# A new order of the same 1088 steps in a one-core RWKV-6 plus SwiGLU kernel

## The chip, the cores and the metric

The kernel runs on one core of a Trainium2 chip. The metric is the device time of one execution in microseconds; lower is better.

## The reference

Inputs are `r`, `k`, `v`, `w` of shape (4, 8, 768, 48) (batch, heads, positions, head size), `u` of shape (8, 48), and the FFN's weights. First a linear attention with a decaying state runs over the 768 positions, then an RMS norm and a SwiGLU FFN:

```python
for t in range(S):
    cur = einsum('bhd,bhe->bhde', u[None] * k_t, v_t)
    y[:, :, t] = einsum('bhd,bhde->bhe', r_t, state + cur)
    state = w_t[:, :, :, None] * state + einsum('bhd,bhe->bhde', k_t, v_t)
x = y.transpose(0, 2, 1, 3).reshape(3072, 384)
xn = x / sqrt(mean(x * x) + 1e-6) * rms_g          # per row
g = xn @ w_gate                                     # 384 x 1536
out = (silu(g) * (xn @ w_val)) @ w_out              # 1536 x 384
```

All data in DRAM is float32; the matmuls run in bfloat16.

## The kernel before

The positions are cut into 6 superblocks `m` of 128. In a superblock, `j` = 0 to 3 are the four batches; a tile (m, j) is 128 positions times 8 heads of 48. The whole program is one list of steps, `PLAN`, that is written out once. Each word of it is a step: `name.m.j` and more indices, `@n` is the buffer or PSUM bank that it takes, and `/A`, `/V`, `/G` says ScalarE, VectorE or GpSimd for steps that can run on any of them. Each engine executes its own steps in the order of the list, and waits by itself for what a step reads and for the buffer that it overwrites. So the list fixes five queues: PE's, VectorE's (DVE), ScalarE's (ACT), GpSimd's (POOL) and that of SyncE (SP), which issues nearly all DMAs.

```python
for step in PLAN.split():
    env.step(step)
```

The steps of a tile (line numbers are those of the profile):

| step | what it does | engine |
|---|---|---|
| `ld.m.j.w/k/r/v` | load of one 192 KB tile (L303) | SP |
| `ln`, `cs`, `exp` | log of the decay, sums of logs along positions by a matmul with a mask (L391), exponential (L400; L397 and L398 for m = 4, 5) | ACT, PE, ACT |
| `rk` | r and k times their decays, to bf16 (L412) | DVE |
| `tr` and `tre`, or `trp` | transposes of that: on PE with a copy out (m = 0, 1), or by DMA for two tiles at once (m from 2 on, L417) | PE and DVE/ACT, or SP |
| `q`, `qm` | r times k for all pairs of positions (L437), causal mask (L440) | PE, DVE |
| `y` | the masked product times v, plus r times the state (L450, L453) | PE |
| `ruk1`, `ruk2`, `bs`, `yd`, `xa` | the term with u and its addition (L478, L482, L485, L490, L494) | POOL, POOL, DVE, POOL, DVE |
| `sq`, `rs`, `xn` | RMS norm of the tile (L498, L503, L364 or L366) | ACT, POOL, any |
| `xt` and `xe`, or `xep` | transpose of the normed tile: on PE with a copy out (m = 0, 1), or by DMA for two tiles (L520) | PE and DVE/ACT, or SP |
| `st`, `sn`, `dk`, `dke`, `dm` | state: k times v (L461), its addition (L467), the decay of the block and its product | PE, DVE, PE, ACT, any |
| `gv.m.g.i.g/v` | gate and value matmuls of block i of the FFN (L538); in m = 0 and 1 for two token groups g of two tiles each, 6 blocks of two columns of 128, later one group, 12 blocks | PE |
| `si`, `hm` | SiLU of the gate (L542), product with the value (L546) | ACT, DVE |
| `o.m.j.q` | a third of the output matmul of a tile (L554) | PE |
| `oo`, `od` | copy out of PSUM, store | DVE/ACT, SP |
| `warm` | a 512-column matmul whose result is not used (L525), 24 of them | PE |
| `tab` | load of ScalarE's function table, for log and exp or for SiLU (L347) | ACT |

The FFN's weights come in float32 as twelve pieces of 384 KB for gate and value (`ldw.p.g`, `ldw.p.h`, p = 2 * third of the rows + half of the columns) and six for the output (`ldwo`). They land in 7 staging slots (`@0` to `@6`) and are cast to bf16 in halves by `wc` and `wco` (L356 to L366); a slot is free for the next piece when both of its halves have been cast. Four of the slots lie in the buffer that holds `hm`'s result of superblock 1.

The inputs have two buffers for each of `w`, `r`/`k` and `v`: superblock m uses one and m + 1 the other, so superblock 1's loads wait for nothing but their turn in SP's queue, and those of m + 2 wait for the last reader of m.

Of the kernel before, what the change touches and what calls it, by code (L numbers as in the profile page):

```python
# [100 lines left out]
tab.le.0 ld.0.1.w@0 ld.0.1.k@0 ld.0.0.r ld.0.3.v@0 ld.0.0.w ln.0.1.1@0 ld.0.2.w ldu cs.0.1@0 ld.0.1.r ld.0.1.v  # L101
ld.0.0.k ln.0.0.1 ld.0.3.r ldg cs.0.0@2 ln.0.2.1 ld.0.3.w ub@4 exp.0.1 ld.0.3.k exp.0.0 vc.0.1.1@0/V ldw.2.h@0
ube/A vc.0.3.1/V rk.0.0@0 ruk1.0.0@0 ldw.5.g@1 rk.0.1 ruk1.0.1@1 tr.0.0@5 ld.0.2.v st.0.1@6 ruk2.0.1 tre.0.0@0/V
ld.0.0.v sn.0.1/A ln.0.3.1 bs.0.1 ldw.0.g@2 cs.0.3@2 wc.2.h.1/V wc.2.h.0/G ld.0.2.r cs.0.2@0 exp.0.3 q.0.0@4
ruk2.0.0 ld.0.2.k vc.0.2.1/A ldw.1.h@3 warm.0@7 ruk1.0.3@1 bs.0.0 exp.0.2 tr.0.1@6 rk.0.3@1 ldw.3.g@4 wc.5.g.1/G
qm.0.0@0 tre.0.1/A tr.0.3@2 ldw.4.h@5 yd.0.0@0 vc.0.0.1/A tre.0.3@1/V q.0.1@4 ldw.0.h@6 wc.0.g.0/A yd.0.1@1
rk.0.2 tab.si.1 warm.1 ruk2.0.3 ldw.1.g@0 q.0.3@2 qm.0.1@1 st.0.3@6 y.0.0@0 wc.0.g.1/G wc.5.g.0/A tr.0.2@1
wc.1.h.1/A xa.0.0@0 ldw.3.h@1 y.0.1@4 st.0.2@5 warm.2 xa.0.1@1 sq.0.0 ruk1.0.2@0 st.0.0@0 warm.3 wc.3.g.1/V
warm.4 sq.0.1 warm.5 warm.6 ruk2.0.2 warm.7 tre.0.2/A warm.8 qm.0.3@2 warm.9 ldw.5.h@2 rs.0.0 wc.1.h.0/A
wc.4.h.0/V wc.4.h.1/G q.0.2@2 xn.0.0@0/A ldw.4.g@3 bs.0.3 warm.10 wc.3.g.0/V y.0.3@4 xt.0.0@1 warm.11 rs.0.1  # L110
ldwo.0@5 bs.0.2 xn.0.1/A wc.1.g.0/V ldw.2.g@4 yd.0.2@2 xe.0.0@0/V wc.0.h.0/A wc.3.h.0/V xt.0.1@1 warm.12
yd.0.3@3 wc.1.g.1/A warm.13 qm.0.2@0 warm.14 xe.0.1/A ldwo.2@0 gv.0.0.4.g@1 ld.1.0.v@1 xa.0.3@2 warm.15
# [12 lines left out]
cs.1.0@0 vc.1.1.1/V o.0.1.0@7 rk.1.1@2 exp.1.0 cs.1.3@2 dke.1@0 rk.1.0 cs.1.2@4 dm.1.0/G tr.1.1@6 ld.2.1.k
exp.1.2 o.0.1.1 bs.1.1 ruk1.1.2@1 tre.1.1@2/V exp.1.3 tr.1.0@0 ld.2.3.r o.0.1.2 vc.1.2.1/V yd.1.1@4 tre.1.0/A
ld.1.3.v o.0.3.0@1 rk.1.2@1 dm.1.3/G ld.2.3.v rk.1.3 q.1.1@4 yd.1.0@0 ld.2.0.k qm.1.1@1 q.1.0@2 tr.1.3@6
dm.1.1/G tr.1.2@0 ld.2.2.r ruk2.1.2 o.0.3.1 qm.1.0@2 tre.1.2@0/A ld.2.3.w@0 o.0.2.0@4 dm.1.2/G tre.1.3/V
oo.0.1@1/A y.1.1@5 ld.2.0.r o.0.3.2 vc.1.3.1/A ruk1.2.1@0 xa.1.1@0 y.1.0@0 ld.2.2.k bs.1.2 sq.1.1 q.1.2@2
xa.1.0@1 oo.0.3@2/A rs.1.1 q.1.3@6 od.0.1 st.1.0@5 qm.1.2@0 sq.1.0 o.0.2.1 xn.1.1@0/A rs.1.0 o.0.2.2 qm.1.3@1  # L130
ruk1.1.3@1 xn.1.0/A xt.1.1@0 y.1.2@1 xe.1.1@1/A xt.1.0@2 ld.2.1.w ruk2.1.3 y.1.3@3 tab.si.2 xe.1.0/V st.1.1@0
ld.2.0.w gv.1.0.2.g@2 yd.1.2@1 bs.1.3 gv.1.0.2.v@6 ld.2.2.v si.1.0.2@0 yd.1.3@3 xa.1.2@3 gv.1.0.1.v@7 ld.3.3.w@1
sq.1.2 gv.1.0.4.g@2 ruk1.2.0@1 xa.1.3@2 gv.1.0.0.g@1 hm.1.0.2@1 ld.2.2.w sq.1.3 ruk2.2.1 oo.0.2@1/V gv.1.0.1.g@3
si.1.0.4@2 ld.2.3.k gv.1.0.3.g@6 rs.1.3 si.1.0.1@1 od.0.0 gv.1.0.0.v@4 ruk2.2.0 si.1.0.0@0 hm.1.0.1 gv.1.0.5.g@2
ld.3.1.w hm.1.0.0 rs.1.2 si.1.0.3@1 st.1.3@3 ld.3.0.w gv.1.0.3.v@1 xn.1.3@1/G sn.1.1 si.1.0.5@0 bs.2.1 st.1.2@4
tab.le.2 o.1.1.0@7 ld.3.2.w sn.1.0 ruk1.2.2@0 gv.1.0.4.v@6 hm.1.0.3 ld.3.2.k@1 ln.2.0.4@0 xt.1.3@0 gv.1.0.5.v@2
xn.1.2/G hm.1.0.4 bs.2.0 hm.1.0.5 xe.1.3/A ruk1.2.3@1 cs.2.0@5 sn.1.3 cs.2.1@0 exp.2.0 ld.3.1.k dk.2@2 sn.1.2
exp.2.1 rk.2.0@0 cs.2.3@3 ld.3.2.r o.1.1.1 dke.2@1 rk.2.1 exp.2.3 ld.2.1.v cs.2.2@5 dm.2.3/G o.1.0.0@2 exp.2.2
rk.2.3@2 trp.2.0@1 dm.2.2/G xt.1.2@0 o.1.1.2 xe.1.2/A ruk2.2.2 rk.2.2 tab.si.3 gv.1.1.1.g@1 ruk2.2.3 trp.2.1@2
gv.1.1.0.g@3 si.1.1.1@1 gv.1.1.2.g@0 dm.2.0/G bs.2.3 gv.1.1.1.v@6 oo.1.1@0/V si.1.1.2@2 dm.2.1/G gv.1.1.2.v@4  # L140
bs.2.2 od.1.1 si.1.1.0@0 hm.1.1.1 ruk1.3.2@1 gv.1.1.0.v@5 vc.2.0.4@0/A ld.3.1.v@1 hm.1.1.2 gv.1.1.3.g@7 yd.2.0@2
ld.3.1.r hm.1.1.0 q.2.0@0 si.1.1.3@1 yd.2.2@4 q.2.1@3 od.0.3 gv.1.1.4.g@6 qm.2.0@2 yd.2.1@0 gv.1.1.5.g@5
ld.3.3.v si.1.1.4@2 qm.2.1@0 y.2.0@7 ld.3.0.k yd.2.3@1 si.1.1.5@0 q.2.3@0 tab.le.3 q.2.2@5 xa.2.0@0 gv.1.1.3.v@3
qm.2.3@1 y.2.1@4 ruk1.3.1@0 sq.2.0 o.1.0.1 ld.3.0.v xa.2.1@1 ln.3.0.4@1 y.2.3@7 rs.2.0 qm.2.2@2 o.1.0.2 ld.3.2.v
st.2.1@4 sq.2.1 xa.2.3@2 ld.3.3.k y.2.2@0 xn.2.0@0/V gv.1.1.5.v@1 rs.2.1 sq.2.3 xa.2.2@3 ld.3.3.r gv.1.1.4.v@5
xn.2.1/V rs.2.3 sq.2.2 hm.1.1.5 cs.3.3@6 ld.3.0.r oo.1.0@0/A rs.2.2 o.1.3.0@0 hm.1.1.3 exp.3.3 xn.2.2@1/G sn.2.1
cs.3.1@1 xep.2.0@0 dk.3@3 hm.1.1.4 exp.3.1 st.2.0@4 o.1.3.1 xn.2.3/V dke.3@0 sn.2.0 xep.2.1 o.1.2.0@5
vc.3.0.4@1/A dm.3.1/G rk.3.1@1 cs.3.0@3 o.1.2.1 ruk2.3.1 rk.3.3@0 od.0.2 exp.3.0 o.1.3.2 dm.3.0/G bs.3.1
# [473 lines left out]
```

## Time and profile before

| | |
|---|---|
| four runs | 209.62, 208.83, 209.03, 211.1 us |
| median | 209.32 us |
| the profiled execution | 209.62 us |
| its span in the profile | 207.8 us, so 1.8 us lie around it |
| busy in the span | PE 189.2, DVE 151.5, ACT 132.8, POOL 115.7 us |
| DMA | 36.75 MB, 129497 packets, of these 123969 under 512 bytes |
| granted TensorE clock | 0.997 |

The profile is of one execution. A line of its timeline has start and duration in us, engine, source line, operation, what is written and read, the count, and in brackets how long the engine idled before and what it waited for. "SPq" are SyncE's DMA issues; a row for them lasts as long as the issue, not as the transfer. A row of the table by stretches has the length, then for PE, PE's weight loads, DVE, ACT and POOL the busy time and count, then the granted clock, the DMA engines' busy share and GB/s. The chain of waits has start, duration and what the end waited for in that time.

### The profile page before, as it was taken

To read this page: it belongs to the slowest core of one execution; us is meant where nothing else is said; L and a number is where in the kernel's file an instruction comes from. 1 tells how busy PE (TensorE), PEld (TensorE's weight loads), DVE (VectorE), ACT (ScalarE), POOL (GpSimd) and SP (SyncE) were. 2 spreads that over 40 slices of the span, in tenths; PEclk is the share of its full clock that TensorE was granted. 3 is DMA by queue.
4 is the path that set the end of the run, shared out by engine and by line. 5 is a ranking of instruction groups with operands and counts; after the bars stand their busy time and mean duration, and the time that the engine had idled before them with its cause. 6 is when DMAs were issued, how large, how long until landed. Compare 5 with 4: busy or idle time off the path is not lost.

```text
span 207.8 us, 4431 instructions
## 1 busy us (share of the span) xinstructions
PE 189.2 (91%) x1642; PEld 117.5 (57%) x1642; DVE 151.5 (73%) x252; ACT 132.8 (64%) x240; POOL 115.7 (56%) x144
## 2 busy tenths in 40 slices
PE   1437979899999989999999999999999999999993
PEld 0124738787677857876445565455664555544461
DVE  2065898477997798998999967799988986023731
ACT  3427778379748899899536988649994753333500
POOL 3059983053598969779866979739965141000000
PEclk9999999999999999999999999999999999999998
DMA  6999989999999997989999999999666307121113
GB/s 126 211 256 271 372 294 246 286 230 211 219 186 236 203 195 136 219 159 210 187 216 206 207 239 204 188 188 246 140 129 134 95 2 69 35 84 44 38 41 115
DMA packets 129497, 36.75 MB, mean 177 GB/s; under 512 B 123969, under 2 KB 127170, under 8 KB 129474
## 3 DMA queue, kind: packets, MB, share of 16 engines
q1 hardware_dynamic: 128928, 36.35, 79.1%
q8 instruction: 13, 0.21, 0.4%
q10 hardware_dynamic: 546, 0.10, 0.3%
q14 instruction: 10, 0.08, 0.1%
HBM read 25.96 MB, written 4.72 MB: 148 GB/s over the span
## 4 chain that ended last, share of the span: by engine, by line
PE 67%; DMA 9%; DVE 9%; SPq 8%; issue 3%; ACT 3%; POOL 1%; DVEq 0%; ACTq 0%; POOLq 0%
PE ps L538 38%; PE ps L554 18%; SPq L303 7%; DMA ht<-in_moe_w_out_dram 3%; PE ps L437 3%; DVE rkA L412 3%; DMA rkT<-rkA 2%; DMA ht<-in_moe_w_val_dram 2%; DMA in_rk<-in_r_dram 2%; PE ps L453 2%; DVE qts L440 2%; PE ps L391 1%; PE ps L450 1%; PE ps L461 1%; PE ps L425 1%
## 5 line engine op out<-in xcount | busy, mean ns | idle before, releaser
L542 ACT ACTIVATE sg<-ps 128x512 bf16<-128x512 f32 x72 | 41.9, 595 | 38.5 <-PE ps L538 27.8
L546 DVE TENSOR_TENSOR ht<-ps,sg 128x512 bf16<-128x512 f32 x72 | 47.8, 685 | 23.3 <-PE ps L538 16.9
L538 PE MATMUL ps<-xnt,wg 128*128 128x256 bf16 (+1 forms) x288 | 54.5, 326 | 0.5 <-ACT xnt L360 0.4
L538 PE MATMUL ps<-xnt,wv 128*128 128x256 bf16 (+1 forms) x288 | 54.7, 326 | 0.0
L554 PE MATMUL ps<-wo,ht 128*128 128x384 bf16 x288 | 53.3, 326 | 0.0
L478 POOL TENSOR_TENSOR ruk<-in_rk 128x384 f32<-128x384 f32 x24 | 24.2, 1011 | 28.4 <-DMA in_rk<-in_k_dram 19.4
L538 PEld LDWEIGHTS <-wg 128*128 128x128 bf16 x288 | 27.6, 98 | 18.0 <-issue 1.0
L538 PEld LDWEIGHTS <-wv 128*128 128x128 bf16 x288 | 27.2, 98 | 16.9
L554 PEld LDWEIGHTS <-ht 128*128 128x128 bf16 x288 | 26.9, 98 | 17.2 <-issue 0.2
L440 DVE TENSOR_TENSOR qts<-ps,mask_lt 128x1024 bf16<-128x1024 f32 x24 | 28.5, 1216 | 0.2 <-PE ps L437 0.2
L482 POOL TENSOR_TENSOR ruk<-ruk,u_bc 128x384 f32<-128x384 f32 x24 | 24.2, 1013 | 0.5
L412 DVE TENSOR_TENSOR rkA<-in_rk,ps 128x768 bf16<-128x768 f32 x24 | 22.2, 948 | 3.1 <-POOL in_rk L408 1.3
L503 POOL TENSOR_TENSOR rstd<-rstd,mhalf 128x1 f32<-128x1 f32 x24 | 13.8, 579 | 16.1 <-ACT junk L498 15.9
L490 POOL TENSOR_TENSOR ydr<-in_v,diag 128x384 f32<-128x384 f32 x24 | 19.7, 839 | 1.7 <-DVE diag L485 1.7
L472 POOL TENSOR_TENSOR st<-sf,wcr 128x384 bf16<-128x384 f32 x19 | 16.0, 845 | 6.4 <-ACT wcr L384 3.4
L498 ACT ACTIVATE junk<-xb 128x388 bf16<-128x388 bf16 x24 | 12.6, 524 | 6.8 <-DVE xb L494 6.4
L485 DVE TENSOR_REDUCE diag<-ruk 128x8 f32<-128x384 f32 x24 | 13.0, 545 | 4.2 <-POOL ruk L482 4.2
L347 ACT ACT_TABLE_LOAD x12 | 15.4, 1283 | 0.9 <-PEq L606 0.7
L494 DVE TENSOR_TENSOR xb<-ps,ydr 128x384 bf16<-128x384 f32 x24 | 13.1, 552 | 2.7 <-PE ps L453 2.2
L391 PE MATMUL ps<-lw,mask_nge 128*128 128x384 bf16 x16 | 5.8, 365 | 9.1 <-ACT lw L350 8.8
L400 ACT ACTIVATE ps<-ps 128x768 f32<-128x768 f32 x16 | 12.4, 793 | 2.4 <-PE ps L391 2.3
L350 ACT ACTIVATE lw<-in_w 128x384 bf16<-128x384 f32 (+1 forms) x12 | 9.8, 838 | 5.6 <-DMA in_w<-in_w_dram 5.5
(79 smaller groups left out, 211.4 us busy)
## 6 DMA issues: line engine op xcount, KB each, us to landing
in_w<-in_w_dram SPq DMA_DIRECT2D x24, 192.0 KB, 3.8
in_rk<-in_k_dram SPq DMA_DIRECT2D x24, 192.0 KB, 3.8
in_rk<-in_r_dram SPq DMA_DIRECT2D x24, 192.0 KB, 3.9
in_v<-in_v_dram SPq DMA_DIRECT2D x24, 192.0 KB, 3.9
out_dram<-obr SPq DMA_DIRECT2D x23, 192.0 KB, 2.7
ht<-in_moe_w_val_dram SPq DMA_DIRECT2D x4, 384.0 KB, 4.7
ht<-in_moe_w_gate_dram SPq DMA_DIRECT2D x4, 384.0 KB, 5.0
ht<-in_moe_w_out_dram SPq DMA_DIRECT2D x4, 384.0 KB, 4.8
```

The source lines that it names most:

```text
L303: self.nc.sync.dma_start(out=t, in_=getattr(self, w)[j, :, m * L:(m + 1) * L, :].rearrange("h t d -> t h d"))
L347: self.nc.scalar.preload_act_table_set(LN_EXP if kind == "le" else SILU)
L412: self.nc.vector.tensor_tensor(out=self.half("rkA", m, j)[:, :, :, 0:D], in0=self.in_rk[:, self.slot["in_rk", m], j], in1=self.b2(("cs", m ...
L440: self.nc.vector.tensor_tensor(out=self.qts[:, self.slot["qts", m, j]].rearrange("p a q t -> p (a q) t"), in0=self.b2(("qb", m, j)).rearra ...
L472: (self.nc.vector if eng == "DVE" else self.nc.gpsimd).tensor_tensor(out=self.st[:, m % 2, j].rearrange("p q (a d) -> p q a d", a=2), in0= ...
L478: self.nc.gpsimd.tensor_tensor(out=self.ruk[:, self.slot["ruk", m, j]], in0=rk[:, 0], in1=rk[:, 1], op=ALU.mult)
L482: self.nc.gpsimd.tensor_tensor(out=t, in0=t, in1=self.u_bc, op=ALU.mult)
L490: self.nc.gpsimd.tensor_tensor(out=self.ydr[:, self.slot["ydr", m, j]], in0=self.in_v[:, self.slot["in_v", m], j], in1=self.diag[:, m * SB ...
L538: self.nc.tensor.matmul(ps[:, a * n:(a + 1) * n].rearrange("p (u t) -> p u t", t=L), lhsT=w[:, c, f * 128:(f + 1) * 128], rhs=x[:, :, c], ...
L542: self.nc.scalar.activation(out=self.sg[:, self.slot["sg", m, g, i]], in_=self.b1(("gvb", m, g, i, "g")), func=AF.Silu)
L546: self.nc.vector.tensor_tensor(out=self.ht[:, self.slot["ht", m], fs[0]:fs[-1] + 1, t0:t0 + n], in0=self.b1(("gvb", m, g, i, "v")).rearran ...
L554: self.nc.tensor.matmul(ps, lhsT=self.ht[:, self.slot["ht", m], f, j * L:(j + 1) * L], rhs=self.wo[:, f, :], start=(f == 0), stop=(f == FC ...
```

## The change

The list of steps is replaced by another order of exactly the same 1088 steps: the former order was taken as the start of a search that went on for 900 seconds more, without building a first order anew from a list of priorities. Nothing else in the program differs. What changes with it: the order on each of the five queues, the bank or buffer of many steps, and the engine of 69 steps (for example `xn.0.0`, `xn.0.1` from ACT to DVE, `tre.0.0`, `tre.0.3` from DVE to ACT, `vc.0.0.1` from ACT to DVE, and 16 of the 24 `wc`). By engine, DVE has 9 `wc` instead of 11, 2 `tre` instead of 4, 14 `xn` instead of 10; ACT has 12 `wc` instead of 9; POOL has 3 `wc` instead of 4 and 5 `xn` instead of 7.

The diff of the head, up to the first `gv`:

```diff
-tab.le.0 ld.0.1.w@0 ld.0.1.k@0 ld.0.0.r ld.0.3.v@0 ld.0.0.w ln.0.1.1@0 ld.0.2.w ldu cs.0.1@0 ld.0.1.r ld.0.1.v
-ld.0.0.k ln.0.0.1 ld.0.3.r ldg cs.0.0@2 ln.0.2.1 ld.0.3.w ub@4 exp.0.1 ld.0.3.k exp.0.0 vc.0.1.1@0/V ldw.2.h@0
-ube/A vc.0.3.1/V rk.0.0@0 ruk1.0.0@0 ldw.5.g@1 rk.0.1 ruk1.0.1@1 tr.0.0@5 ld.0.2.v st.0.1@6 ruk2.0.1 tre.0.0@0/V
-ld.0.0.v sn.0.1/A ln.0.3.1 bs.0.1 ldw.0.g@2 cs.0.3@2 wc.2.h.1/V wc.2.h.0/G ld.0.2.r cs.0.2@0 exp.0.3 q.0.0@4
-ruk2.0.0 ld.0.2.k vc.0.2.1/A ldw.1.h@3 warm.0@7 ruk1.0.3@1 bs.0.0 exp.0.2 tr.0.1@6 rk.0.3@1 ldw.3.g@4 wc.5.g.1/G
-qm.0.0@0 tre.0.1/A tr.0.3@2 ldw.4.h@5 yd.0.0@0 vc.0.0.1/A tre.0.3@1/V q.0.1@4 ldw.0.h@6 wc.0.g.0/A yd.0.1@1
-rk.0.2 tab.si.1 warm.1 ruk2.0.3 ldw.1.g@0 q.0.3@2 qm.0.1@1 st.0.3@6 y.0.0@0 wc.0.g.1/G wc.5.g.0/A tr.0.2@1
-wc.1.h.1/A xa.0.0@0 ldw.3.h@1 y.0.1@4 st.0.2@5 warm.2 xa.0.1@1 sq.0.0 ruk1.0.2@0 st.0.0@0 warm.3 wc.3.g.1/V
-warm.4 sq.0.1 warm.5 warm.6 ruk2.0.2 warm.7 tre.0.2/A warm.8 qm.0.3@2 warm.9 ldw.5.h@2 rs.0.0 wc.1.h.0/A
-wc.4.h.0/V wc.4.h.1/G q.0.2@2 xn.0.0@0/A ldw.4.g@3 bs.0.3 warm.10 wc.3.g.0/V y.0.3@4 xt.0.0@1 warm.11 rs.0.1
-ldwo.0@5 bs.0.2 xn.0.1/A wc.1.g.0/V ldw.2.g@4 yd.0.2@2 xe.0.0@0/V wc.0.h.0/A wc.3.h.0/V xt.0.1@1 warm.12
-yd.0.3@3 wc.1.g.1/A warm.13 qm.0.2@0 warm.14 xe.0.1/A ldwo.2@0 gv.0.0.4.g@1 ld.1.0.v@1 xa.0.3@2 warm.15
...
+tab.le.0 ld.0.2.w@0 ld.0.1.w ld.0.0.w ld.0.1.k@0 ld.0.0.r ln.0.2.1@0 ld.0.3.w ldu ln.0.1.1 ld.0.3.v@0 cs.0.1@0
+ln.0.0.1 ld.0.2.k cs.0.2@2 ld.0.0.k exp.0.2 ld.0.1.v ub@4 ln.0.3.1 ld.0.3.r cs.0.0@6 ld.0.1.r exp.0.0 ld.0.3.k
+ldg exp.0.1 rk.0.0@0 ruk1.0.0@0 ld.0.2.v ube/V vc.0.1.1@0/A cs.0.3@6 ld.0.2.r ruk2.0.0 tr.0.0@5 exp.0.3
+ldw.0.h@0 rk.0.1 ruk1.0.1@1 tre.0.0@0/A ldw.5.g@1 rk.0.3@1 tr.0.1@4 ruk2.0.1 ldw.2.h@2 q.0.0@0 bs.0.1 tre.0.1/A
+ld.0.0.v vc.0.2.1/V ruk1.0.3@1 warm.0@5 vc.0.3.1/A ldw.0.g@3 qm.0.0@0 tr.0.3@6 tab.si.1 yd.0.1@0 ldw.1.g@4
+rk.0.2 ruk2.0.3 q.0.1@0 tre.0.3@1/A ldw.4.g@5 wc.0.h.0/V wc.5.g.0/G warm.1 bs.0.0 wc.0.h.1/A tr.0.2@7 ldw.3.g@6
+qm.0.1@1 wc.5.g.1/A ruk1.0.2@0 wc.2.h.0/A ldw.4.h@0 vc.0.0.1/V y.0.1@4 wc.2.h.1/A yd.0.0@1 xa.0.1@0 y.0.0@6
+ldw.2.g@1 st.0.3@2 ruk2.0.2 bs.0.3 warm.2 sq.0.1 warm.3 st.0.1@3 tre.0.2/V q.0.3@0 rs.0.1 xa.0.0@1 yd.0.3@2
+qm.0.3@2 q.0.2@6 sq.0.0 warm.4 warm.5 wc.0.g.0/A warm.6 ldwo.3@2 rs.0.0 warm.7 warm.8 wc.0.g.1/A xn.0.0@0/V
+xn.0.1/V xt.0.0@4 wc.1.g.0/A wc.4.g.1/V ldw.1.h@3 xt.0.1@0 warm.9 xe.0.0@0/V y.0.3@1 wc.3.g.0/A bs.0.2 warm.10
+st.0.2@4 warm.11 xe.0.1/A wc.4.h.0/V warm.12 wc.4.g.0/V warm.13 wc.3.g.1/A gv.0.0.3.g@0 wc.1.g.1/V ldw.3.h@5
...
```

SP's queue from the transposes of superblock 2 to those of superblock 3, read out of the two lists:

```
before: trp.2.0 trp.2.1 od.1.1 ld.3.1.v ld.3.1.r od.0.3 ld.3.3.v ld.3.0.k ld.3.0.v ld.3.2.v ld.3.3.k ld.3.3.r
        ld.3.0.r xep.2.0 xep.2.1 od.0.2 ld.4.1.k ld.4.0.k trp.3.0 trp.3.1
new:    trp.2.0 ld.3.1.k trp.2.1 ld.3.3.w ld.3.1.r ld.3.0.v ld.3.0.k od.1.1 ld.3.3.v ld.3.1.v ld.3.2.v od.0.2
        ld.3.3.r xep.2.0 ld.3.0.r xep.2.1 od.0.3 ld.4.0.k trp.3.0 trp.3.1
```

PE's order around `cs` of superblock 2:

```
before: xt.1.3 gv.1.0.5.v cs.2.0 cs.2.1 dk.2 cs.2.3 o.1.1.1 cs.2.2 o.1.0.0 xt.1.2 o.1.1.2 gv.1.1.1.g
new:    gv.1.0.4.v xt.1.3 cs.2.0 o.1.1.1 cs.2.1 cs.2.3 cs.2.2 dk.2 o.1.1.2 gv.1.1.2.g
```

On SP's queue, the last tile of superblock 3's `w` moves from place 70 of the 154 issues to place 77, and that of superblock 5 from 127 to 129 (counted from 0).

## The prediction

> **What bounds the kernel now.** I read the page first, then the busy time by stretch, then the instructions in order of time around the first FFN matmul, SyncE's DMA issues, and the chain of waits between 86 and 108 us. The page's second part:
>
> ```profile
> span 207.8 us, 4431 instructions
> ...
> PE   1437979899999989999999999999999999999993
> ...
> DMA  6999989999999997989999999999666307121113
> ```
>
> A slice is 5.2 us: PE is nearly full from the ninth on, and the DMA engines are full up to the 29th. The stretches say how much PE idles (first pair of numbers: length, PE busy):
>
> ```profile
> 0.00:31.00 31.00, 17.95 (x139) 10.22 (x140) 17.83 (x36) 17.15 (x29) 19.45 (x30) 1.00 0.97 256
> 31.00:100.00 69.00, 66.98 (x731) 51.82 (x729) 57.90 (x100) 54.84 (x96) 46.20 (x56) 1.00 0.97 210
> 100.00:204.30 104.30, 104.25 (x777) 55.48 (x774) 75.43 (x117) 60.51 (x114) 50.06 (x59) 1.00 0.65 134
> ```
>
> Idle PE is 13.05 us before 31 us, 2.02 us from there to 100 us, 0.05 us to the last matmul, and 3.5 us of output tail. The PE work is the same multiset of matmuls in both orders, so a reordering moves the end only by (a) the moment at which gv starts, (b) what PE work is left then, (c) the idle of the middle, at most 2 us to win, and (d) new stalls. The first gv:
>
> ```profile
> 30.16 0.46 ACT L360 COPY xnt<-ps 128x384 bf16<-128x384 bf16 x1
> ...
> 30.67 0.70 PE L538 MATMUL ps<-xnt,wg 128*128 128x256 bf16 x5 [0.44 <-ACT xnt L360]
> ```
>
> It waits for xe.0.1, not for a weight. The second bound is SyncE's queue, which issues every load in order: between 31 and 146 us it waits for data for only 0.4 us and then once more, before trp.2.0:
>
> ```profile
> 74.61 0.70 SPq L303 DMA_DIRECT2D in_v<-in_v_dram  x1
> 78.46 2.01 SPq L417 DMA_TRANSPOSE rkT<-rkA  x1
> ```
>
> That gap is 3.15 us. Elsewhere a load is late because the queue is full. The chain shows where this touches PE:
>
> ```profile
> 92.24 3.91 DMA in_rk<-in_r_dram
> ...
> 96.18 0.96 DVE rkA L412
> ...
> 102.52 4.33 DMA rkT<-rkA
> ...
> 106.90 0.40 PE ps L437 x8
> ```
>
> The last r tile of superblock 3 lands, rk and the DMA transpose follow, and q.3.2 starts as that transpose lands. A new order has to win at the head and must not lose it in this queue.
>
> **1. The head, up to the first gv.** Landings come one per 1.05 us (27 transfers from 3.48 to 30.67 us; 0.99 for the first twelve small ones, about 1.1 for a 384 KB weight). The new queue puts 15 of the 16 tiles of superblock 0 ahead of the weights, so I place: k00 11.4 us (as now), r01 14.4 (now 9.4), r02 17.3, then 0.h, 5.g, 2.h at 18.4 to 20.5, v00 21.2 (now 18.1), 3.g 25.7.
>
> VectorE, with start-to-start times of the rows (rk 0.87, qm 1.14, bs, xa and sn 0.47, tre 0.61, wc 0.33): rk.0.1 waits for r01 to 15.4, qm.0.0 17.3 to 18.5, qm.0.1 20.1 to 21.3, xa.0.1 22.5, xa.0.0 24.05; sq.0.0 (0.62) and rs.0.0 (0.6) bring xn.0.0 and xn.0.1, now both on VectorE, to 26.0. In the trace xn.0.1 is a ScalarE step that ends at 29.18, after rs.0.1 waited behind the 1.28 us cast wc.4.h.1 on GpSimd. Before xe.0.0, VectorE loses three weight casts (1.0 us), one tre (0.6) and bs.0.2 (0.5), and gains the two xn and ube (0.9). ScalarE casts 0.g, 1.g.0 and 3.g.0 (0.54 each) after sq.0.0 and ends xe.0.1 at 27.3. The first gv (0.0.3.g) needs 1.g.0, 3.g.0 and 5.g.0: all cast by 26.9.
>
> On PE, seven warm matmuls, y.0.3, st.0.2, xt.0.0 and xt.0.1 lie between q.0.2 (24.7) and gv, so their speed counts. [...] Row:
>
> ```profile
> 24.48 0.63 PE L525 MATMUL ps<-mask_lt 128*128 128x512 bf16 x1
> ...
> 25.23 1.97 PE L525 MATMUL ps<-mask_lt 128*128 128x512 bf16 x7
> ```
>
> The first of these spends 0.63 us, those after about 25.6 us come every 0.22. If this change of speed comes at 25.6 again, gv starts at **28.3**. [...] I take the row: 28.3, **-2.4 us**. [...]
>
> **2. Work left over.** st.0.0 and one more warm now come after the first gv: 0.17 + 0.22 = **+0.4**.
>
> **3. Middle, 31 to 75 us.** Stalls that go: 0.68 at 38.69 (VectorE stood before wco.5.0, waiting for its DMA, with xn.0.3 queued behind it; that cast is now ScalarE's), 0.34 at 57.88, and 0.73 + 0.2 + 0.2 around cs.2.0 to cs.2.2. What is late next, by the same walk: q.1.0 waits 0.2 for rk.1.3 and tre.1.0; cs.2.0 0.15 for ln.2.0 behind its table load; cs.2.2 now takes the bank of cs.2.0 and waits 0.6 for rk.2.0. Together 2.15 go and 0.95 come: **-1.2**. Bounds: 0 and -1.8. All of superblock 1's loads come without one of superblock 2 among them, the last (v12) at about 53.5 against 58.9 now, so ln.1.2 and rk.1.3 still find their data, by 1 us.
>
> [...] The trace shows both: the cast wc.3.h.0 took 0.95 beside GpSimd's yd.0.2, but wc.3.g.0 took 0.41 wholly inside GpSimd's wc.4.h.1. The new order has wc.1.g.1 on VectorE begin inside wc.2.g.1 on GpSimd (27.9 to 29.15), with qm.0.2 behind it and y.0.2 waiting. [...] The other swaps between engines (obr copies, vc, rw, dm) lie where PE has work queued, and cost nothing while that cover holds; without it each costs at most its own length, 0.3 to 1.5 us, once.
>
> **4. Superblock 2 to 3, on SyncE's queue.** Here the order loses. A load (31k) now stands between trp.2.0 and trp.2.1, and the last r tile (30r) comes behind xep.2.0 instead of ahead of it. With L for the lead gained so far: rk.2.3 ends at 81.1 - L, trp.2.1 has been issued at 83.9 - L (2.6 us each in this stretch), ten items follow as one per 1.0 us, xep.2.0 is reached at 93.9 - L, 30r is issued at 95.3 - L, and xep.2.1 at 96.3 - L lands (3.1 to 3.3) at 99.5 - L. gv.2.0.5.g follows st.3.0, which waits for rk.3.0 on 30r: about 100.2 - L, against 99.01 for the first gv.2.0 now. **+1.2**; ends 0 and +2. From there to the end both orders have 0.05 us or less to lose: y.5.0 to gv.5 has 9.3 us of other matmuls between, where the trace's chain took 7.6. **0**.
>
> Sum: -2.4 + 0.4 - 1.2 + 1.2 = -2.0. Against the profiled execution's own 209.62 (span 207.8 and 1.8 around it) that is 207.6; this execution lay 0.3 above the median of the four (209.32), so **207.3** as a median, 1.0% less. About 1% is also what a measurement of this kernel can tell from no change.
>
> **Rivals.**
> - *The queue gives nothing back* (step 4 is free, because 30r and the transposes find shorter queues as the DMA engines catch up): 207.3 - 1.2 = **206.1**. For it: in the trace SyncE waited 3.15 us at trp.2.0, so there is slack ahead of the place. Against: from trp.2.1 to xep.2.0 there was none.
> [...]
> - *v00 stops VectorE, slower.* vc.0.0.1 moves from ScalarE to VectorE and v00 from 16th to 19th transfer, behind three weights. VectorE has no spare time from there to the first gv; sq.0.0 follows, ScalarE's casts of 0.g are behind it, and ldw.1.h, which needs their stage slot, then blocks SyncE with all later loads behind it. Each us that v00 lands after 21.3 costs one us. At 1.05 us a transfer it lands in time; the gain is gone at 23.3 (1.10 us each), and at 1.2 to 1.25 us each, 25.6 us, the kernel is at 207.3 + 4.3 = **211.6**. For it: the last weights of the trace (4.g, 2.g) came 1.2 to 1.5 apart with stalls. Against: small tiles took 0.75 to 1.0.
> - That the change does not do what it says is no case here: only the list of steps changes.
>
> **How the numbers follow.** Forecast case 0.43, free queue 0.17, late speed-up 0.17, v00 0.23. The forecast lies at the edge of 1%: about half of its cases and all of the free queue are faster by over 1% (0.40), the other half, most of the late speed-up and a little of v00 are within 1% (0.37), and v00 is slower (0.23). The range takes in the free queue with the earliest gv (205.6) and the nearer half of the v00 case: 205.6 to 211.2.
>
> **What would show it.** Right: first gv at 27.9 to 29.6 us with xt.0.1 done before 28; v00 landing near 21.3; 31 to 75 us with about 1 us of idle PE; the first gv.2.0 at 96 to 97.5 us, waiting for rk.3.0 or for xnt by DMA, and SyncE waiting about 2 us before trp.2.0. Wrong: first gv after 30.7, idle PE of more than 1 us after 100 us, a wait at cs.3 or cs.5 for ln (their last w tiles now come late in the queue), or ScalarE as the releaser of long waits in the head.

## The result, and the profile after

| | old order | new order |
|---|---|---|
| median | 210.01 us (64 runs, 208.28 to 211.55) | 210.85 us (43 runs, 208.74 to 212.78) |
| profiled execution | 209.62 us | 210.78 us |
| its span | 207.8 us | 209.0 us |
| its last matmul ends at | 204.30 us | 204.41 us |
| from there to the end of the span | 3.54 us | 4.58 us |

The ratio of new to old is **1.0033** (95% interval 1.0017 to 1.0049): slower by a third of a per cent, where 1% less was forecast. Ratios are formed from the fast executions of each kernel alone, so they are not the quotients of the medians. The last two rows are the first finding: in this pair of executions the last matmul ends 0.11 us later, and 1.04 of the 1.16 us that were lost lie behind it, in a part that the prediction took as given.

The page of the new order (5.2 us to a digit, as before):

```profile
span 209.0 us, 4424 instructions
...
PE   0638789999999989999999999999999999999991
...
DMA  6999969999899969989999999899584303212022
```

The stretches that were shown of the old order, now of the new one (length, then busy time and count of PE, PE's weight loads, DVE, ACT, POOL, then granted clock, DMA share, GB/s):

```profile
0.00:31.00 31.00, 18.69 (x142) 11.14 (x143) 18.39 (x36) 19.10 (x31) 18.22 (x29) 1.00 0.93 247
31.00:100.00 69.00, 66.88 (x727) 51.18 (x727) 58.95 (x100) 57.13 (x100) 42.86 (x54) 1.00 0.99 216
100.00:204.30 104.30, 103.91 (x774) 55.23 (x772) 75.75 (x119) 56.37 (x110) 52.65 (x60) 1.00 0.62 132
```

PE does 0.74 us more before 31 us, idles 2.12 us instead of 2.02 in the middle, and 0.39 us instead of 0.05 after 100 us. The first gv starts at 28.78 us against 30.67; the idle PE after it sums to 3.26 us against 2.07. The timeline of the new order around it (start, length, engine, line, operation, what is written and read, count, and the idle time before with what ended it):

```profile
27.53 0.48 ACT L360 COPY xnt<-ps 128x384 bf16<-128x384 bf16 x1 [0.26 <-PE ps L513]
...
28.42 1.55 DVE L366 TENSOR_SCALAR wg<-stage_x,g_col 128x384 bf16<-128x384 f32 x2
...
28.78 0.82 PE L538 MATMUL ps<-xnt,wg 128*128 128x256 bf16 x6
...
28.83 0.92 POOL L490 TENSOR_TENSOR ydr<-in_v,diag 128x384 f32<-128x384 f32 x1
...
29.89 1.21 DVE L440 TENSOR_TENSOR qts<-ps,mask_lt 128x1024 bf16<-128x1024 f32 x1
...
31.15 0.81 PE L538 MATMUL ps<-xnt,wg 128*128 128x256 bf16 x6 [0.90 <-DVE qts L440]
```

xe.0.1 ends at 28.0 us and gv follows at 28.78 without idle PE: st.0.2 and three warm matmuls stand between. Then comes a new stall. The two casts on VectorE are wc.4.g.0 and wc.1.g.1; the second takes 0.98 us beside GpSimd's yd.0.2, so qm.0.2 ends at 31.10, and gv.0.0.0.g, which takes the bank that qm.0.2 reads, waits 0.90 us.

After 100 us there is one stall, and it comes from SyncE's queue:

```profile
127.01 3.01 SPq L417 DMA_TRANSPOSE rkT<-rkA  x1
...
130.06 0.58 SPq L562 DMA_DIRECT2D out_dram<-obr  x1
...
134.23 0.48 ACT L360 COPY obr<-ps 128x384 f32<-128x384 f32 x1 [2.77 <-DMA out_dram<-obr]
...
134.76 0.81 PE L538 MATMUL ps<-xnt,wv 128*128 128x512 bf16 x3 [0.39 <-ACT obr L360]
```

The issue of trp.4.0 lasts 3.01 us; the store od.1.3 stands behind it, lands at 134.20, and oo.2.0, which needs its buffer, holds ScalarE for 2.77 us and PE for 0.39.

### The profile page after: what moved, and what is told of

The parts are those of the page before. It is cut to its first block, busy times and chain, and to the rows that moved or that the text cites. A ratio compares the mean times of both kernels' runs of the same rounds, so it can differ in the third digit from the quotient of the medians.

```text
span 209.0 us, 4424 instructions
## 1 busy us (share of the span) xinstructions
PE 189.6 (91%) x1642; PEld 117.6 (56%) x1642; DVE 153.5 (73%) x253; ACT 132.9 (64%) x242; POOL 113.7 (54%) x141
## 4 chain that ended last, share of the span: by engine, by line
PE 65%; SPq 11%; DVE 9%; DMA 7%; ACT 3%; issue 2%; POOL 1%; DVEq 0%; POOLq 0%; ACTq 0%
PE ps L538 38%; PE ps L554 17%; SPq L303 11%; DMA in_rk<-in_r_dram 4%; DVE qts L440 3%; PE ps L437 2%; PE ps L525 2%; DMA out_dram<-obr 2%; DMA in_v<-in_v_dram 2%; PE ps L391 2%; PE ps L453 1%; DVE rkA L412 1%; PE ps L450 1%; PE ps L461 1%; ACT ps L400 1%
## 5 line engine op out<-in xcount | busy, mean ns | idle before, releaser
L542 ACT ACTIVATE sg<-ps 128x512 bf16<-128x512 f32 x72 | 41.6, 597 | 37.7 <-PE ps L538 27.4
L538 PE MATMUL ps<-xnt,wg 128*128 128x256 bf16 (+1 forms) x288 | 55.3, 326 | 0.9 <-DVE qts L440 0.9
L538 PE MATMUL ps<-xnt,wv 128*128 128x256 bf16 (+1 forms) x288 | 55.7, 326 | 0.4 <-ACT obr L360 0.4
L554 PE MATMUL ps<-wo,ht 128*128 128x384 bf16 x288 | 52.3, 326 | 0.0
L478 POOL TENSOR_TENSOR ruk<-in_rk 128x384 f32<-128x384 f32 x24 | 25.0, 1042 | 23.0 <-DMA in_rk<-in_k_dram 15.4
L412 DVE TENSOR_TENSOR rkA<-in_rk,ps 128x768 bf16<-128x768 f32 x24 | 22.7, 950 | 15.6 <-DMA in_rk<-in_k_dram 8.6
L482 POOL TENSOR_TENSOR ruk<-ruk,u_bc 128x384 f32<-128x384 f32 x24 | 24.7, 1037 | 0.9 <-DVE u_bc L356 0.6
L503 POOL TENSOR_TENSOR rstd<-rstd,mhalf 128x1 f32<-128x1 f32 x24 | 13.3, 556 | 18.2 <-ACT junk L498 17.7
L490 POOL TENSOR_TENSOR ydr<-in_v,diag 128x384 f32<-128x384 f32 x24 | 20.2, 850 | 3.8 <-DVE diag L485 3.8
L472 POOL TENSOR_TENSOR st<-sf,wcr 128x384 bf16<-128x384 f32 x18 | 15.1, 850 | 9.0 <-ACT wcr L384 4.5
L356 DVE COPY obr<-ps 128x384 f32<-128x384 f32 (+1 forms) x11 | 5.8, 535 | 13.1 <-PE ps L554 13.1
```

Source lines behind the costliest of these rows:

```text
L412: self.nc.vector.tensor_tensor(out=self.half("rkA", m, j)[:, :, :, 0:D], in0=self.in_rk[:, self.slot["in_rk", m], j], in1=self.b2(("cs", m ...
L472: (self.nc.vector if eng == "DVE" else self.nc.gpsimd).tensor_tensor(out=self.st[:, m % 2, j].rearrange("p q (a d) -> p q a d", a=2), in0= ...
L478: self.nc.gpsimd.tensor_tensor(out=self.ruk[:, self.slot["ruk", m, j]], in0=rk[:, 0], in1=rk[:, 1], op=ALU.mult)
L482: self.nc.gpsimd.tensor_tensor(out=t, in0=t, in1=self.u_bc, op=ALU.mult)
L490: self.nc.gpsimd.tensor_tensor(out=self.ydr[:, self.slot["ydr", m, j]], in0=self.in_v[:, self.slot["in_v", m], j], in1=self.diag[:, m * SB ...
L538: self.nc.tensor.matmul(ps[:, a * n:(a + 1) * n].rearrange("p (u t) -> p u t", t=L), lhsT=w[:, c, f * 128:(f + 1) * 128], rhs=x[:, :, c], ...
```

## Experiments

The runs of one group share a chip and the runs of the old order on it; each ratio is to those. The old order's median was 209.63, 209.36, 211.34, 210.09 and 210.90 us on the five chips, so times of different groups are not set side by side.

### Cutting the list

At many places the first n steps of one list can be followed by the other list's remaining steps, with one to three buffers renumbered. Four such kernels, called hybrids here, tell where the time goes:

```diff
 # for example
-PLAN = <new order>
+PLAN = <first 239 steps of the new order> + <all other steps, in the old order>
```

New order to 46 us, then old:

> The new order's first 239 steps (its head and FFN up to 46 us on TensorE), then all other steps in the old order. Theory 'worn down': the two profiles give the new order a lead of 1.1 us of TensorE work at its first gv and 0.85 us at 46 us (it idles 0.90 us before gv.0.0.0.g where the old one idles 0.68 before xt.0.3), which the old order's rest then keeps: about 0.85 us faster than before, ratio 0.996. Rival 'stream': the load stream is full until 145 us and ends at the same time in both, so a lead gained at the head is waited away in the middle: ratio 1.000. Rival 'head is no gain' (one profile is not typical): ratio 1.002 or more.

New order to 97 us, then old:

> The new order's first 557 steps (up to 97 us on TensorE, with the place where the r tile of superblock 3 comes behind xep.2.0), then the old order. 'Worn down': the stalls of the new order between 46 and 97 us (q.1.0, q.1.3, cs.2.0, cs.2.2, q.2.2, cs.3.2, st.3.0: 1.9 us against 1.2 us in the old order) leave a lead of 0.2 us: ratio 0.999 (0.997 to 1.001), and the new order's own loss lies after 97 us. 'Stream': 1.000. If the loss of the new order (1.003) lies before 97 us: 1.003.

Old order to 48 us, then new:

> The old order's first 245 steps (up to 48 us on TensorE), then the new order. 'Worn down': the lead of the new head is missing and its middle costs: new order's 1.0033 plus 0.85 us, ratio 1.006 to 1.008. 'Stream': as the new order, 1.003. 'Head is no gain': 1.001 to 1.002.

Old order to 104 us, then new:

> The old order's first 600 steps (up to 104 us on TensorE), then the new order. What it shows is the price of the new order after 104 us alone. By the profile that is the one stall before gv.3.0.7.v, which waits for oo.2.0 on ScalarE, which waits for the store od.1.3: 0.4 us, ratio 1.002. 'The whole loss lies before 104 us': 1.000. 'The late part varies from run to run and costs over 0.8 us in the middle run': 1.004 or more.

| kernel | ratio (95% interval) | last matmul to end, profile |
|---|---|---|
| new to 46 us, then old | 1.0003 (0.9978 to 1.0027) | 3.54 us |
| new to 97 us, then old | 1.0002 (0.9974 to 1.0030) | 3.88 us |
| old to 48 us, then new | 1.0108 (1.0075 to 1.0141) | 4.59 us |
| old to 104 us, then new | 1.0150 (1.0095 to 1.0205) | 3.90 us |

The first two are the old order's time, as the rival "stream" said and not as "worn down" did: the gain of the head is given back. The profile of the first shows where (SyncE's transposes trp.3.0 and trp.3.1, one row for both, and q.3.2; in these kernels line numbers differ by a few):

```profile
98.01 5.67 SPq L412 DMA_TRANSPOSE rkT<-rkA  x2
...
106.81 0.40 PE L432 MATMUL ps<-rkT 48*128 48x128 bf16 x8 [0.98 <-DMA rkT<-rkA]
```

q.3.2 starts at 106.81 us against 106.90 in the old order, with 0.98 us of idle PE ahead of it instead of 0.05. It is the place of the prediction's chain of waits. The profile alone does not prove that all of the 0.98 us is the lead: the old order with padding (below), which has no lead, waits 0.59 and 0.72 us there in its two profiles. That the gain is given back is what the ratios say.

The last two lost more than any theory said. For the third the place stays open, since its only profile is of the longest of its executions (216.0 us against a median of 212.19). In the fourth the renumbering has a part: its oo.2.2, not oo.2.0, is the first to take the buffer of od.1.3, and stands earlier in ScalarE's queue:

```profile
126.44 3.43 SPq L412 DMA_TRANSPOSE rkT<-rkA  x1
...
129.92 0.58 SPq L557 DMA_DIRECT2D out_dram<-obr  x1
...
132.24 0.48 ACT L355 COPY obr<-ps 128x384 f32<-128x384 f32 x1 [3.59 <-DMA out_dram<-obr]
...
132.77 1.46 PE L533 MATMUL ps<-xnt,wv 128*128 128x512 bf16 x6 [2.17 <-ACT obr L355]
```

So it is not the price of the new order's late part, but it shows what the same store can cost: 2.17 us of PE, of the 3.3 us by which this execution is longer than the profiled one of the old order. The column on the right varies by over a microsecond; the part on the end takes it up.

### Single places

The store od.1.3 ahead of the transpose:

```diff
-trp.4.0@2
...
-gv.3.0.7.g@6 od.1.3 si.3.0.3@0
+od.1.3 trp.4.0@2
...
+gv.3.0.7.g@6 si.3.0.3@0
```

> The new order with one store moved: od.1.3 is issued just ahead of trp.4.0 and no longer behind it. Theory 'store behind the transpose': the new order loses its time after 104 us because trp.4.0 waits for rk.4.2 with od.1.3 queued behind it, and oo.2.0, which needs that store's buffer, stops ScalarE and then TensorE at gv.3.0.7.v (0.39 us in the profile, more in other executions): the stall is gone, ratio to before 0.9995 to 1.0015 instead of 1.0033. Rival 'the loss lies elsewhere': 1.003.

Measured: 1.0017 (0.9990 to 1.0045), and no stall after 100 us in its profile. The ratio moved as expected, but its interval holds 1.0033 too.

The old order without nine warm matmuls:

> The old order without the nine warm matmuls that come after its first gv (warm.15 to warm.23); their results are used by nothing. They are 2.1 us of TensorE work before 55 us. Theory 'stream': TensorE meets the load stream again at q.3.2, which in the old order starts as its transpose lands, so that work saved ahead of it comes back as a wait there: ratio 0.998 to 1.000, with about 1 to 2 us of idle TensorE at q.3.2 or at other consumers of loads. Rival 'TensorE work sets the end': 0.990 to 0.992.

Measured: 1.0041 (1.0007 to 1.0074): slower, which neither theory said. In its profile the saved work came back in full. The waits of PE between 31 and 205 us, first without these matmuls, then in the old order:

```profile
PE ps L507 <- DVE xnr L360: 1.8, 1, 1.8
PE ps L431 <- DVE rkA L406: 0.8, 2, 0.5
PE ps L385 <- ACT lw L344: 0.6, 1, 0.6
PE ps L532 <- ACT xnt L354: 0.5, 1, 0.5
PE ps L431 <- DMA rkT<-rkA: 0.4, 1, 0.4
```

```profile
PE ps L513 <- DVE xnr L366: 0.7, 1, 0.7
PE ps L391 <- ACT lw L350: 0.6, 1, 0.6
PE ps L437 <- DVE rkA L412: 0.3, 1, 0.3
```

PE's work after the first gv falls by 1.76 us, its idle time rises by 1.91 us, 1.1 of it at xt.0.3, which waits for xn.0.3, and 0.4 at q.3.2, which waits for its transpose. Why its ratio is above 1 all the same is not settled.

New order to 46 us, old rest, and q.3.2 behind two gv that wait for nothing:

```diff
-q.3.2@6 qm.3.0@0 gv.2.0.7.v@4 ruk1.4.0@0 gv.2.0.0.g@5
+qm.3.0@0 gv.2.0.7.v@4 ruk1.4.0@0 gv.2.0.0.g@5 q.3.2@6
```

> The new order's first 239 steps and the old order's rest, as in the first run, with q.3.2 moved 1.3 us later on TensorE (behind gv.2.0.7.v and gv.2.0.0.g, which wait for nothing). In the first run q.3.2 gave back 0.98 us of the lead. 'Stream gate at q.3.2': the lead of about 0.9 us passes: ratio 0.9955 to 0.997. Rival 'the next gate takes it' (trp.4.1 to q.4.2, as 0.86 us in the run with the cut at 97 us): 1.000.

The same, and without the ten warm matmuls after the first gv:

> The same, without the ten warm matmuls after the first gv: 2.2 us less TensorE work before 55 us. 'TensorE work sets the end once the gate is open': ratio 0.986 to 0.988. 'Stream': most of it comes back as waits for transposes and loads between 57 and 135 us: 0.995 to 1.000.

Measured: 0.9992 (0.9967 to 1.0018) and 0.9967 (0.9944 to 0.9990). In the first profile q.3.2 waits no more and the last matmul ends at 203.03 us; the second is the first kernel whose interval lies below the old order. It gains 0.0025 on the first, 0.5 us, where its saved work would give 1.4 (172.22 to 170.78 us of PE work after gv).

### The end behind the last matmul

The instructions behind the last matmul are the same steps in both orders, yet the ten profiles fell into groups. Sorted by the number of instructions that the profile records on SyncE and on GpSimd:

| kernel | SyncE, GpSimd | last packet of a store after the last matmul | end of the span after it |
|---|---|---|---|
| old; old without nine warm | 219, 207 | 2.16, 2.15 us | 3.54, 3.52 us |
| the three hybrids cut at 46 us | 218, 206 | 2.16 to 2.17 us | 3.54 to 3.56 us |
| new to 97 us, then old | 220, 202 | 2.15 us | 3.88 us |
| old to 104 us, then new | 215, 207 | 2.16 us | 3.90 us |
| new; new with od.1.3 moved; old to 48 us, then new | 217, 201 | 2.68 to 2.73 us | 4.58 to 4.59 us |

The page's third part has two queues of kind "instruction". Over the last microseconds (203 to 210 us, 0.175 us to a column), first the old order, then the new:

```profile
GB/s 53 334 351 351 35 0 0 0 202 386 395 188 0 0 22 272 242 220 312 57 0 0 0 0 0 0 0 0 0 0 0 0 0 0 0 0 0 0 0 0
...
q14 instruction: 1, 0.01, 0.5%
```

```profile
GB/s 0 140 351 386 246 0 0 0 18 307 404 334 62 0 0 97 316 167 310 237 9 4 26 4 0 0 0 0 0 0 0 0 0 0 47 0 0 0 0 0
...
q14 instruction: 2, 0.02, 0.8%
```

The last hump is the final store in two halves. In the old order it ends at once; in the new one a thin trail follows (9, 4, 26, 4), and at 209.07 us comes one more transfer by itself (47). The packets of the trace tell what these are. (A fetch, from here on, is a packet of 8 KB, 8192 bytes, of the instruction queue q14.)

The trail is a part of the store that came late. A fetch starts 0.71 us after the last matmul in the old order and 1.89 us after it in the new, where it lies among the last store's packets and takes 0.53 us. The store's last eight packets of 768 bytes start as it ends, at 2.41 us. In the other three profiles with a trail they do the same, within 0.02 us of the fetch's end. So the last packet is late because eight packets stood behind a fetch.

The lone transfer is a second fetch. It starts 4.65 us after the last matmul, which is 0.07 us after the end of the span, so nothing in the span waits for its bytes. What comes with it is a delay on GpSimd in the closing handshake, as the last EVENT_SEMAPHORE and DRAIN rows of the engines are called here. A DRAIN there starts 3.94 us after the last matmul instead of 3.04 and lasts 0.23 us instead of 0.08. Of the 0.90 us, 0.61 are the late store; the other 0.29 and the longer duration are 0.44 us. The row of this instruction, first in the old order, then in the new (its middle one of three; shortest, median and longest in ns):

```profile
L617 POOLq DRAIN  x3: 34/78/656, 172.4 to 207.6; - x3
```

```profile
L617 POOLq DRAIN  x3: 34/226/1714, 172.7 to 208.7; - x3
```

What holds GpSimd before that fetch starts is not shown. (So far delay and fetch only go with the counts; the next runs move the counts.)

To move only the counts, padding was put where nothing waits for it:

```diff
+    # GpSimd: six times, behind its last step (about 174 us)
+    nc.gpsimd.memset(pad[:, i:i + 1], 0.0)
+    # SyncE: twice, behind od.4.2
+    nc.sync.dma_start(out=pad[0:1, 8 + 4 * i:12 + 4 * i], in_=u[0:1, 0:4])
```

New order with both, and with the two loads alone:

> The new order, with nothing moved, and two kinds of padding in the last 35 us: six memsets of one column on GpSimd behind its last step, and two loads of 16 bytes on SyncE behind od.4.2; nothing uses what they write. In the profiles so far the time from the last matmul to the end of the span goes with the number of instructions on SyncE and GpSimd, and not with the order: 3.5 us with 218 or 219 on SyncE and 206 or 207 on GpSimd (four kernels), 4.6 us with 217 and 201 (three kernels, the new order among them). Theory 'instruction fetch in the tail': an 8 KB instruction fetch falls on the last store (its last packet at 2.7 us after the last matmul instead of 2.16), and another stops GpSimd in the closing handshake (0.4 us); the padding moves both ahead to a time when they cost nothing: tail 3.5 to 3.6 us and ratio 1.0033 - 0.005 = 0.998 to 0.999. Rival 'the tail differs by chance, or by the order': tail 4.6 us, ratio 1.003.

> The same with the two loads on SyncE alone. 'Instruction fetch': SyncE's fetch moves ahead of the last store, GpSimd's stays: tail 3.9 to 4.0 us. Rival: 4.6 us.

Padding with od.1.3 moved, and padding with wc.1.g.1 moved:

> The padding together with od.1.3 ahead of trp.4.0. If both causes add (0.005 for the tail, 0.0016 for the store): ratio to before 0.996 to 0.998.

> The padded new order with one cast moved: wc.1.g.1 on VectorE behind qm.0.2 instead of ahead of it. In every profile with the new head TensorE idles 0.8 to 1.3 us before gv.0.0.0.g, which takes a bank that qm.0.2 reads; qm.0.2 stood behind wc.1.g.1, which took 0.98 us beside GpSimd's yd.0.2 (0.41 elsewhere). 'The cast is the cause': the stall falls to 0 to 0.2 us. For the end: 'the load stream takes back what is won at the head': as the padded new order (0.998 to 0.999); 'TensorE work sets the end': 0.004 less (0.994).

| kernel | SyncE, GpSimd | last packet | end | ratio (95% interval) |
|---|---|---|---|---|
| new, padded | 219, 207 | 2.15 us | 3.39 us | 0.9945 (0.9918 to 0.9971) |
| new, two loads alone | 219, 201 | 2.15 us | 3.85 us | one execution, no ratio |
| the same as the first, od.1.3 moved | 219, 207 | 2.16 us | 3.39 us | 0.9938 (0.9907 to 0.9969) |
| the same as the first, wc.1.g.1 moved | 219, 207 | 2.16 us | 3.41 us | 0.9942 (0.9919 to 0.9964) |

The ends came nearly as the theory said: the loads take 0.73 us off 4.58 (0.53 of it is the last packet), the memsets 0.46 more, and with each the fetch in question starts earlier (0.78 us after the last matmul instead of 1.89) or is gone from the end. The ratio fell by more than expected, but the unpadded new order was not run on this chip. And **neither move adds to it**: the stall of 0.9 us at gv.0.0.0.g is gone in the last kernel, and its time stays.

### On one chip

> The new order as it is, beside its padded form on the same chip. 'Instruction fetch in the tail': tail 4.6 us, and 1.2 us (0.0055 of the old order's time) slower than the padded form in the next run. Rival 'the padded form was fast only because of that chip': both the same, 1.001 to 1.003.

> The padded new order once more. 'Instruction fetch': tail 3.4 us, ratio 0.0055 under that of the run before: 0.998 if the new order is at 1.0033 here, 0.9945 as last time if the old order is slow on this chip too. Rival: as the run before.

> The padded new order with both moves, od.1.3 ahead of trp.4.0 and wc.1.g.1 behind qm.0.2. 'TensorE work sets the end': 0.9 and 0.4 us less than the padded form, 0.006 under its ratio. 'The load stream takes back what is won at the head': 0.4 us less, 0.002 under it. No difference: the store's stall too is taken back later.

> The fastest hybrid so far (new order to 46 us, old rest, q.3.2 later, no warm matmuls after the first gv: 0.9967) with wc.1.g.1 behind qm.0.2 too, which takes away 0.8 us of idle TensorE at 32 us. 'Stream': 0.996 to 0.997 as before. 'TensorE work sets the end': 0.993.

| kernel | median | ratio (95% interval) | end |
|---|---|---|---|
| old | 210.09 us | | |
| new | 210.15 us | 1.0007 (0.9981 to 1.0032) | 4.75 us |
| new, padded | 209.08 us | 0.9937 (0.9911 to 0.9964) | 3.40 us |
| new, padded, both moves | 208.50 us | 0.9925 (0.9900 to 0.9950) | 3.41 us |
| hybrid without warm, wc.1.g.1 moved | 209.91 us | 0.9985 (0.9957 to 1.0013) | 3.54 us |

The padding is worth 0.0070 of 210 us, 1.5 us, on one chip (the medians of all executions differ by 1.07); the profiles' ends differ by 1.35. The two moves bring 0.0012, inside the intervals. The hybrid's saved 0.8 us at 31 us came back before 55 us, as idle PE ahead of gv.0.1.3.v (1.15 us) and dk.1 (1.63 us). After this idle time its profile also has 3.4 us at half the granted clock (the number before the DMA share), and PE's work after gv is 172.31 us instead of the 170.78 without the move:

```profile
53.15:56.57 3.42, 3.10 (x16) 1.89 (x16) 2.62 (x5) 1.76 (x4) 3.07 (x4) 0.50 1.06 211
```

That is one execution; the move itself does not add work. The new order with padding and both moves has the lowest ratio of the study.

### Controls

> Control: the old order with the same padding (six memsets, two loads). Its fetches already lie clear of the end, so if the padding works only through the place of the instruction fetch, it wins nothing but the 0.14 us by which the padded tails (3.40 us) were shorter than the old order's (3.54): ratio 0.999 to 1.000. Rival 'the padding speeds up any order' (it keeps a queue or an engine awake): 0.993 to 0.995.

The old order with 122 memsets of one column on GpSimd behind its last step, and no loads, which makes 207 + 122 = 201 + 128 instructions on GpSimd:

> [...] 'A block of 128': GpSimd's fetch falls into the closing handshake again: tail 3.9 to 4.0 us instead of 3.54, ratio 1.002. Rival 'only the work done there counts, not the number of instructions': 3.54 us, 1.000.

The old order with the padding of the new: 1.0017 (0.9985 to 1.0049), end 3.40 us: the padding speeds up nothing by itself. The old order with 122 memsets: 329 instructions on GpSimd, end **3.98 us**, ratio 1.0033 (0.9998 to 1.0067), and the lone transfer at the end is there (203 to 210 us, after the last store's hump):

```profile
GB/s 0 0 0 0 0 0 176 404 334 211 0 0 0 61 351 351 372 35 0 0 145 316 145 312 202 4 0 0 0 0 0 0 0 0 0 47 0 0 0 0
...
q14 instruction: 2, 0.02, 0.8%
```

No thin trail follows the hump here; SyncE's count was left at 219. GpSimd was held in the profiles with 201, 202 and 329 instructions on it and not in those with 206 and 207, and 329 is 201 + 128. The step of 128 was the author's estimate, and no other count was tried. For the end of the profile the cause is shown from both sides: six instructions more take GpSimd's delay away from the new order, and 122 more give it to the old one. For the time it is shown from one side: the ratio 1.0033 is not clear of noise, and the profile with 122 memsets also has a wait of PE of 0.37 us at 179.80 that the old order has not.

## Why the prediction was wrong

**The step that failed is the first premise**: that the end moves only by the start of gv, the work left, the idle middle and new stalls, with "3.5 us of output tail" as a constant. The tail went from 3.54 to 4.58 us (4.75 in the second profile). No step of the tail was moved; the new order has fewer recorded instructions on SyncE (217 for 219) and GpSimd (201 for 207), and fetches start 1.89 and 4.65 us after the last matmul, where the old order has one, 0.71 us after it.

It is not the only term that was off. In the pair of profiled executions the terms of the prediction's sum came out so:

| term | forecast | in the pair |
|---|---|---|
| start of the first gv | -2.4 us | -1.9 us |
| PE's work after it | +0.4 us | +0.8 us |
| idle PE from gv to 80 us | -1.2 us | +0.6 us |
| idle PE from 80 to 110 us | +1.2 us | +0.3 us |
| idle PE from 110 us to the last matmul | 0 | +0.4 us |
| behind the last matmul | 0 | +1.0 us |
| sum | -2.0 us | +1.2 us |

The largest single error is the middle (1.8 us), the tail is the next (1.0). The tail is the one that experiments prove: with padding alone the new order stands at 0.9945 and 0.9937 where 0.990 was forecast, so the forecast's side is right and half to two thirds of its gain are there. In the first comparison less would be left: 1.0 to 1.5 us off 1.0033 make 0.996 to 0.998 (an estimate). For the middle the cause below is read from profiles; taking its longest stall away won nothing that can be measured.

Step by step:

1. *The head, -2.4 us.* Right in kind, a little less. The first gv came between 28.2 and 30.2 us in 14 profiles with the new head, mean 28.9; the old head's came between 30.5 and 31.3. So -2.0. v00 landed at 20.9 to 22.0 us, where 21.2 was placed: the rival in which it stops VectorE is out. The spread goes with the clock. At half clock the warm matmuls follow each other every 0.40 to 0.43 us, at full clock every 0.22. One profile of the new head in three stretches (the granted clock is the number before the DMA share; the trace's record of the clock starts with the first stretch at full clock, so the column says 1.00 for all that lies before, slow or not):

```profile
19.62:23.03 3.41, 1.55 (x28) 1.04 (x27) 3.41 (x7) 2.79 (x6) 3.41 (x4) 1.00 1.07 386
23.03:26.45 3.42, 3.31 (x26) 1.70 (x25) 3.10 (x7) 2.46 (x8) 2.61 (x4) 0.50 1.05 407
26.45:31.00 4.55, 3.65 (x39) 2.63 (x38) 4.08 (x8) 2.47 (x6) 3.55 (x3) 1.00 0.67 192
```

In the 14 profiles the full clock that lasted through gv began between 25.2 and 28.7 us. Where it began after 27.4 us (5 of the 14) gv started at 29.1 or later, otherwise at 28.2 to 28.9. In all 20 profiles, of both heads, the lasting full clock begins 3.5 to 6.8 us after PE's last idle stretch of over 1.2 us. What sets the place in this range is not shown. The row that was taken (25.6) was one draw near the early end of what the 14 profiles show. For the 27.9 and 29.6 us that the prediction names for the first gv, for the 205.6 us at the low end of its range and for the 0.17 given to a late speed-up no run shows a source; the runs showed 28.2 to 30.2 us.
2. *Work left over, +0.4.* The steps were counted rightly; PE's time after gv rose by 0.82 us in the pair of profiles, of which these two steps are 0.39. The rest is spread thin. Such work ahead of 55 us is worth little here: nine matmuls less won nothing.
3. *The middle, -1.2.* Wrong in sign: +0.6 in the pair. By PE's idle time 1.58 us of stalls went (0.68, 0.34 and 0.56); the prediction reckoned 2.15 from start to start. The new waits that it listed came as computed: 0.25 for 0.2 at q.1.0, 0.19 for 0.15 at cs.2.0 and 0.57 for 0.6 at cs.2.2. But 0.90 and, at q.1.3, 0.26 came besides, 2.17 in all instead of 0.95. The term that was missed is the cast wc.1.g.1 on VectorE beside GpSimd: the sum has nothing for it, and it became 0.90 us of PE. The cast came beside yd.0.2, not beside the cast wc.2.g.1, so of the prediction's two rows the one beside yd.0.2 (0.95) was the nearer, not the one inside a cast (0.41). Of the 192 weight casts on VectorE in all profiles, those beside which GpSimd ran nothing took 0.40 to 0.42 us (48 casts). Those that lay for 70% of their time or more beside one instruction of GpSimd took 0.40 to 0.42 beside rs (32), 0.40 to 0.77 beside a cast (28), 0.80 to 0.91 beside ruk2 (14) and 0.95 to 0.99 beside yd (13). Where yd was still running as the cast began, the cast ended 0.22 us after it (15 casts; 29.55 against 29.33 us in the old order, 29.97 against 29.75 in the new). Beside GpSimd's own casts that is not so: a cast of 0.76 us ended 0.45 us before the one on GpSimd. In the kernel's time the stall was worth nothing measurable all the same.
4. *Superblock 2 to 3, +1.2.* The places came nearly as computed. With L = 1.5 us, the lead that the new order had at cs.2.0 (73.77 against 75.21 us), the load 30r was due at 93.8 and came at 93.5, gv.2.0.5.g was due at 98.7 and came at 98.5. (The prediction's own lead was larger, so that it looked for the first gv.2.0 at 96 to 97.5.) But PE idled only 0.6 us between 80 and 110 us, against 0.3: other matmuls stood ahead. So the price was 0.3, not 1.2, and this error hides half of that of step 3.
5. *From there to the end, 0.* Not 0: od.1.3 behind trp.4.0. Order on SyncE's queue was looked at only up to superblock 3; this store is the same kind of mistake that the prediction warned of, one superblock later. It cost PE 0.39 us in this profile, 0.33 to 0.55 in three of the padded profiles, and nothing in the second profile of the new order.

For step 4 the rival of the free queue (206.1) was nearer to what was measured. What the hybrids add: in the old order's queue the lead of the new head is gone by the end (1.0003), and the profile points to the DMA transpose at q.3.2. Moving that step (0.9992), or saving work in the old order (1.0041), shows no gain; both in the hybrid show a small one (0.9967). The new order's own queue lets about 1.2 us through (0.9944, the padded ratio with the 0.14 us of its shorter handshake put back; 0.6 to 1.7 by its interval).

Open: what holds GpSimd in the handshake, where the time goes that taking single stalls away should have won, why the new order stands at 1.0033 in the first comparison and at 1.0007 on the chip of the fourth group, and why the old order without nine warm matmuls is slower rather than equal.

## What to carry to other kernels

Read the stretch behind the last compute instruction as a stage of its own, in both profiles, before explaining a difference of a per cent by the work ahead of it: here 1.1 us of it went with a count of instructions. When two orders of the same work differ by less than 1%, compare the instruction fetches near the end, and if one falls there, move it with a few idle instructions (six memsets and two loads here: 4.58 to 3.39 us). A lead at the head is not yet a gain at the end: ask of each later step that waits for a transfer when that transfer lands, down to the last store whose buffer is used again. And one profile is one draw: here the first gv moved by 2 us between executions of one head.

## What was not expected of the hardware

- Instruction fetches show up in the DMA queues and can cost time. One of 8 KB among the last store's packets put the last packet from 2.16 us to 2.7 or 2.8. Where another came at the very end, GpSimd (201, 202 or 329 instructions) was held in the closing handshake for 0.3 to 0.4 us, and in one kernel SyncE (215 instructions) for 0.36 us, before that fetch itself began.
- The same head starts lasting full-speed matmuls (one every 0.22 us) anywhere from 25.2 to 28.7 us from one execution to the next, and the first gv moves with it by 2 us (28.2 to 30.2). In all 20 profiles they started 3.5 to 6.8 us after PE's last idle stretch of over 1.2 us.
